# Wider channel-mixing spans and smaller fp32 tiles in a polynomial-attention mixer kernel

## The chip, the cores and the metric

One core of a Trainium2 chip runs the whole program. The metric is the device time of one execution in microseconds; the kernel before took 226.24 (median of 3 runs, 225.53 to 226.71). Five engines work side by side: TensorE (PE, with its weight loads listed apart as PEld), VectorE (DVE), ScalarE (ACT), GpSimd (POOL) and SyncE (SP), which issues the DMAs here.

## The reference

Attention with products of two learned projections in place of exponentials, followed by a mixer of tokens and channels. Batch is 4, heads 4, sequence 1088, head size 32, model width 128.

```
def phi(x):                                  # S1, S2: 8 x 32
    a = einsum('rd,bhsd->bhsr', S1, x)
    b = einsum('rd,bhsd->bhsr', S2, x)
    return outer(a, b).reshape(..., 64)
kv  = einsum('bhsf,bhsd->bhfd', phi(k), v)   # per head 64 x 32
z   = sum(phi(k), axis=2)
x   = einsum(phi(q), kv) / (einsum(phi(q), z) + 1e-6)
x   = x, heads side by side                  # B x 1088 x 128
h   = relu(x.T @ w_tok1) @ w_tok2            # tokens, 1088 -> 256 -> 1088
u   = x + h.T
out = u + relu(u @ w_ch1) @ w_ch2            # channels, 128 -> 1536 -> 128
```

## The kernel before

All work on features lies transposed, 128 model columns on the partitions. The four batches go one after the other through these steps; the planner names operations by step and batch (K1 is the keys of batch 1).

- **Weights.** The mixer's weights arrive as 64-bit floats in pieces of up to 512 columns. `convert` (lines 337 to 376) makes 32-bit words of each piece: two passes on ScalarE (L347, L351), three on VectorE (clamp L354, shift L358 by way of a PSUM bank of tag ps_h, merge L361) and an addition on GpSimd (L365, L367). `divide_weight` then splits the words into a high and a low fp32r half (L448 on ScalarE, L451 on GpSimd).
- **Keys, K.** L478 projects the keys: for each 64 rows one fp32 matmul, 64 weight columns, 64 columns of result. ScalarE copies one factor out (L488), VectorE multiplies the outer products (L497). L514 sums them against v with a column of ones: 64 features of one head as weights, the 66 columns of two heads as stream. L524 copies the wanted diagonal blocks into kvz, a block-diagonal matrix for two heads.
- **Queries, Q.** Batch 0 projects on PE with spread matrices (L593), and the product is made on VectorE (L614) or GpSimd (L611). Batches 1 to 3 project 16 rows per head (L559), write them to DRAM (L653), read them back repeated (L666, L669), and multiply in place (L679).
- **Attention and tokens, A.** L699 multiplies 64 tokens of phi(q) for two heads with kvz (66 columns). VectorE divides: L710 adds the small constant, L711 takes the reciprocal, L713 multiplies. Then come the token products (L749 in fp32 for batch 0, L755 in fp32r halves after it), relu, a transpose (L789), and the second product (L871, L875). u is split into halves uh and ul (L846, L849).
- **Channels, U.** The 4352 columns of all batches are cut in spans: 384, 384 and 320 for batch 0, then eight of 384 and one of 192 that run across batches. For each span and each of 12 pieces of 128 hidden channels, L925 makes the hidden values with three fp32r matmuls (high by high, high by low, low by high), ScalarE writes relu as the high half hh (L929), VectorE the rest hl (L932), and L938 adds three matmuls into the span's bank of tag ps_o. L957 or L963 adds u, and L974 stores.

An fp32 matmul appears in the trace as two passes, each with its weight load; one of fp32r as one. The buffers hid, hh and hl have four copies each, u, uh and ul four, the PSUM tags ps_a and ps_h three banks and ps_o two.

What runs when is settled ahead: `Plan.run` (lines 191 to 265) holds every operation with a cost per engine and picks, at each moment of its own clock, the ready operation with the highest level. The table LEAD raises or lowers some levels by hand, PBIAS keeps work off VectorE where GpSimd could take it, and gaps on PE longer than FILL are filled with matmuls of the identity (L326). Each engine then runs its own list in order.

The reason for splitting into spans is one line; another sets the attention's bank and columns:

```
for n in (384,) * 8 + (192,):
...
x_ps[c:c + 64, o:o + 2 * (D + 1)],
lhsT=qp[:, p, s0 + c:s0 + c + 64], rhs=kvz_all[b % 2][:, p, :], start=True, stop=True,
```

Of the kernel before, what the change touches and what calls it, by code (L numbers as in the profile page):

```python
# [18 lines left out]
P = 128  # L19
# [17 lines left out]
WIDE = 384  # L37


def _spans():  # L40
    spans = [((0, c0, cn),) for c0, cn in CHUNKS]
    at = S
    for n in (384,) * 8 + (192,):
        parts = []
        while n:
            b, c = divmod(at, S)
            m = min(n, S - c)
            parts.append((b, c, m))
            at, n = at + m, n - m
        spans.append(tuple(parts))  # L50
# [8 lines left out]
HID = 4  # L59
# [3 lines left out]
LEAD = {  # L63
    "A0.u2": -92200.0,
    "A0.ul00": 52700.0,
    "A0.x0": 25900.0,
    "A1.hT": -8500.0,
    "A2.t2": -139200.0,
    "A2.uh06": -39900.0,
    "A2.w1": 10800.0,  # L70
    "A3.t2": 42400.0,
    "A3.uh08": -24000.0,
    "A3.w1": -196200.0,
    "A3.x": -343500.0,
    "K0.c0": 176700.0,
    "K1.c0": 32500.0,
    "K2.c4": 181200.0,
    "Q0.p00": 649300.0,
    "Q0.p01": 151600.0,
    "Q0.p10": -11700.0,  # L80
    "Q0.p20": 167900.0,
    "Q0.p21": -40200.0,
    "Q1.m01": -15400.0,
    "Q3.p": -57100.0,
    "U0.f": 304500.0,
    "U1.f": 86500.0,
    "U11.f": 700.0,
    "U4.f": -200.0,
    "U6.f": -92300.0,
    "U7.f": -14400.0,  # L90
    "U8.f": -30200.0,
    "w00.hi": -545600.0,
    "w00.lo": -70200.0,
    "w01.hi": -76700.0,
    "w01.lo": -95600.0,
    "w02.add": -21200.0,
    "w02.clamp": -28000.0,
    "w02.hi": -51200.0,
# [12 lines left out]
    "w13.abs": 35300.0,
    "w13.clamp": -72500.0,
    "w13.hi": 21300.0,
    "w14.clamp": 29000.0,
    "w14.low": -26800.0,
    "w15.abs": -433000.0,
    "w15.clamp": 5100.0,
    "w15.low": -39400.0,
    "w20.abs": 69100.0,
    "w20.clamp": -38500.0,  # L120
    "w20.low": 61500.0,
    "w21.clamp": 7900.0,
    "w21.low": -32300.0,
    "w22.abs": -73200.0,
    "w22.low": -647900.0,
    "w30.abs": 8700.0,
    "w31.hi": -263000.0,
    "w32.abs": -118900.0,
    "w32.add": 25400.0,
    "w32.lo": -77700.0,  # L130
    "w32.low": -17200.0,
}
# [4 lines left out]
PBIAS = 1300.0  # L137
# [6 lines left out]
STICK = 3000.0  # L144
# [6 lines left out]
def f32(ap):  # L151
    return ap.bitcast(F32)
# [17 lines left out]
class Plan:  # L170
# [20 lines left out]
    def run(self, fill):  # L191
        for op in reversed(self.ops):
            cost = op.weight if op.weight is not None else min(op.ways.values()) + LATE.get(min(op.ways, key=op.ways.get), 0)
            op.level = cost + max((n.level for n in op.next), default=0.0)
        for op in self.ops:
            op.level += op.boost + LEAD.get(op.name, 0.0)
        free = dict.fromkeys(LATE, 0.0)
        free["sp"], free["act"], free["pe"] = 1060.0, 2000.0, 1400.0 + 427 * WARM
        dma, mode = 2800.0, 0

        port = 0.0
        waiting = {op: len(op.before) for op in self.ops}
        ready = [op for op in self.ops if not op.before]
# [6 lines left out]
        while ready:  # L210
            best = []
            for op in ready:
                t = max((a.end for a in op.after), default=0.0)
                ok = True
                for k, h in enumerate(op.takes):
                    q = self.taken.setdefault(h.pool, [])
# [7 lines left out]
                if not ok:  # L224
                    continue
# [819 lines left out]
```

## Time and profile before

| what | value |
|---|---|
| median of 3 runs | 226.24 us |
| span of the profiled execution | 224.5 us (its only time; the median lies 1.7 above) |
| busy: PE, DVE, ACT, POOL | 218.0, 142.7, 117.5, 80.0 us |
| granted TensorE clock | 1.00 (0.99 in the last 12.5 us) |
| moved by DMA | 28.41 MB, mean 127 GB/s |
| first channel-mixing pass | at 32.12 us |
| last matmul, last DVE instruction | start at 221.09 and 221.40 us |

In the chain of waits each row is a stretch: where it starts, how long it lasts, which engine's work it is, with the tile and line, and after an x how many instructions. A row of the timeline gives start, length, engine, line, operation, destination and sources, and in brackets how long the engine was idle before it and what ended that. A group row gives busy time and the mean of one instruction behind the bar. Busy time of PE is modelled where matmuls are pipelined, so the distance between starts says more than the length of one.

### The profile page before, as it was taken

The numbers are of one execution on the slowest core, as the hardware profiler recorded it, in microseconds if no ns is written. First come the engines' busy times: TensorE is split into PE (matmuls) and PEld (weight loads), VectorE is DVE, ScalarE is ACT, GpSimd is POOL, SyncE is SP. The second block draws the span as 40 slices with busy tenths as digits, with TensorE's granted clock in tenths as the row PEclk, the third lists the DMA queues.
The fourth block names the chain that finished last, engine by engine and source line by source line (L and its number), as shares of the span: only waits on it lengthen the run. The fifth ranks groups of instructions, "written<-read, shape, count | busy, mean of one in ns | idle before, by whom it ended". The sixth has DMA issues, their size and how long they took to land.

```text
span 224.5 us, 4803 instructions
## 1 busy us (share of the span) xinstructions
PE 218.0 (97%) x1860; PEld 204.5 (91%) x1860; DVE 142.7 (64%) x285; ACT 117.5 (52%) x271; POOL 80.0 (36%) x85
## 2 busy tenths in 40 slices
PE   7999999989999999999999999999999999999994
PEld 7667778869999999899999999999999999999994
DVE  1599989999578745366443755773375556556562
ACT  4597679986426153354443554343254554444451
POOL 2256589899997352243440230050020300000000
PEclk9999999999999999999999999999999999999999
DMA  5999995997419643038760000124000000101000
GB/s 175 418 404 403 405 355 173 208 197 233 156 33 220 196 158 105 32 67 202 222 206 3 3 35 0 38 105 105 3 35 1 35 3 2 33 0 39 0 35 18
DMA packets 10726, 28.41 MB, mean 127 GB/s; under 512 B 1360, under 2 KB 4688, under 8 KB 10704
## 3 DMA queue, kind: packets, MB, share of 16 engines
q1 hardware_dynamic: 10704, 28.11, 39.6%
q8 instruction: 14, 0.23, 0.4%
q14 instruction: 8, 0.07, 0.1%
HBM read 23.27 MB, written 4.83 MB: 125 GB/s over the span
## 4 chain that ended last, share of the span: by engine, by line
PE 78%; DMA 15%; DVE 3%; ACT 1%; SPq 1%; POOL 0%; issue 0%; POOLq 0%
PE ps_o L938 31%; PE ps_h L925 31%; DMA br<-rows 4%; PE ps_a L755 4%; DMA doubles<-wt 4%; PE ps_a L875 4%; DMA doubles<-wc 4%; PE ps_a L699 3%; DMA q_sb<-qT 3%; PE ps_a L514 2%; PE ps_a L871 1%; DVE hl L932 1%; PE ps_a L478 1%; DVE ps_h L358 1%; PE ps_o L326 0%; PE ps_a L789 0%
## 5 line engine op out<-in xcount | busy, mean ns | idle before, releaser
L932 DVE SCALAR_TENSOR_TENSOR hl<-ps_h,hh 128x384 fp32r<-128x384 f32 (+2 forms) x144 | 75.4, 533 | 53.6 <-ACT hh L929 53.3
L929 ACT ACTIVATE hh<-ps_h 128x384 fp32r<-128x384 f32 (+2 forms) x144 | 68.0, 474 | 69.4 <-PE ps_h L925 65.0
L925 PE MATMUL ps_h<-uh,halves 128*128 128x384 f32 (+2 forms) x288 | 89.8, 334 | 1.1 <-DVE hl L932 1.1
L938 PE MATMUL ps_o<-hh,halves 128*128 128x384 f32 (+2 forms) x288 | 71.7, 331 | 0.0
L925 PEld LDWEIGHTS ps_h<-uh,halves 128*128 128x128 f32 x288 | 53.6, 188 | 3.0 <-DVE hl L932 2.0
L938 PEld LDWEIGHTS ps_o<-hh,halves 128*128 128x128 f32 x288 | 50.5, 188 | 0.4
L925 PE MATMUL ps_h<-ul,halves 128*128 128x384 f32 (+2 forms) x144 | 47.5, 330 | 0.0
L938 PE MATMUL ps_o<-hl,halves 128*128 128x384 f32 (+2 forms) x144 | 47.3, 328 | 0.0
L925 PEld LDWEIGHTS ps_h<-ul,halves 128*128 128x128 f32 x144 | 27.1, 188 | 0.4 <-DVE ul L849 0.2
L938 PEld LDWEIGHTS ps_o<-hl,halves 128*128 128x128 f32 x144 | 27.1, 188 | 0.0
L849 POOL TENSOR_TENSOR ul<-us,uh 128x320 fp32r<-128x320 f32 (+5 forms) x15 | 9.4, 652 | 41.5 <-ACT uh L846 41.4
L679 POOL TENSOR_TENSOR qp<-qp,br 128x544 f32<-128x544 f32 x12 | 16.2, 1365 | 16.9 <-DMA br<-rows 16.9
L723 POOL TENSOR_TENSOR xl<-x,xh 128x384 fp32r<-128x384 f32 x9 | 9.1, 1016 | 20.4 <-ACT xh L719 20.4
L365 POOL TENSOR_TENSOR whole<-c,tail 128x512 int32<-128x512 int32 (+3 forms) x11 | 11.7, 1071 | 11.4 <-DVE c L361 11.4
L347 ACT ACTIVATE c<-doubles 128x512 f32<-128x512 f32 (+3 forms) x17 | 10.7, 627 | 4.0 <-POOL whole L365 2.6
L451 POOL TENSOR_TENSOR halves<-whole,halves 128x512 fp32r<-128x512 f32 (+3 forms) x11 | 11.8, 1093 | 0.2 <-ACT halves L448 0.2
L354 DVE TENSOR_SCALAR c<-c 128x512 f32<-128x512 f32 (+3 forms) x17 | 10.0, 612 | 2.9 <-ACT c L347 2.8
L497 DVE TENSOR_TENSOR k_p<-ps_a,a_sb 128x1024 f32<-128x1024 f32 (+1 forms) x12 | 10.9, 948 | 0.3 <-ACT a_sb L488 0.3
L699 PEld LDWEIGHTS ps_a<-kvz,qp 128*64 128x64 f32 x288 | 8.9, 137 | 1.9 <-issue 1.2
L361 DVE SCALAR_TENSOR_TENSOR c<-doubles,ps_h 128x512 int32<-128x512 int32 (+3 forms) x17 | 10.4, 610 | 0.2
L358 DVE TENSOR_SCALAR ps_h<-c 128x512 int32<-128x512 int32 (+3 forms) x17 | 10.2, 614 | 0.1
L351 ACT ACTIVATE tail<-doubles 128x512 int32<-128x512 uint32 (+3 forms) x17 | 10.0, 613 | 0.0
(76 smaller groups left out, 238.9 us busy)
## 6 DMA issues: line engine op xcount, KB each, us to landing
qp<-rows SPq DMA_DIRECT2D x6, 544.0 KB, 10.8
br<-rows SPq DMA_DIRECT2D x12, 272.0 KB
doubles<-wc SPq DMA_DIRECT2D x6, 512.0 KB, 9.5
v_sb<-v SPq DMA_DIRECT2D x4, 594.0 KB, 7.5
k_sb<-kT SPq DMA_DIRECT2D x4, 576.0 KB, 5.3
q_sb<-qT SPq DMA_DIRECT2D x4, 544.0 KB, 14.0
doubles<-wt SPq DMA_DIRECT2D x4, 512.0 KB, 9.8
xm<-xb SPq DMA_DIRECT2D x3, 576.0 KB, 2.8
```

Source lines behind the costliest of these rows:

```text
L347: nc.scalar.activation(f32(t["c"]), f32(high), AF.Abs)
L358: nc.vector.tensor_scalar(t["ps"], t["c"], 3, 0x3FFFFFFF, op0=ALU.logical_shift_left, op1=ALU.bitwise_and)
L361: nc.vector.scalar_tensor_tensor(t["c"], high, -(1 << 30), t["ps"], op0=ALU.bitwise_and, op1=ALU.bitwise_or)
L365: engines[e].tensor_tensor(dst(), t["c"], t["tail"], op=ALU.add)
L451: engines[e].tensor_tensor(halves[w, i][:, 1], f32(whole[w, i] if w < 2 else t["c"]), f32(halves[w, i][:, 0]), op=ALU.subtract)
L497: nc.vector.tensor_tensor(t["k_p"][:pn, t0 * H:t1 * H], a.unsqueeze(3).broadcast_to([pn, n, R, R]), t["sb", t0][:pn, :n].unsqueeze(2).broa ...
L679: engines[e].tensor_tensor(qp[:, p, cs], qp[:, p, cs], t["br"][:, p, cs], op=ALU.mult)
L699: nc.tensor.matmul(x_ps[c:c + 64, o:o + 2 * (D + 1)], lhsT=qp[:, p, s0 + c:s0 + c + 64], rhs=kvz_all[b % 2][:, p, :], start=True, stop=True,)
L925: nc.tensor.matmul(h_ps[:, :cn], lhsT=part(2, at[2][e][0], l, at[2][e][1] * P, P), rhs=r[:, :cn], start=(m == 0), stop=(m == 2))
L929: nc.scalar.activation(t["hh"][:, :cn], t["h"][:, :cn], AF.Relu)
L932: nc.vector.scalar_tensor_tensor(t["hl"][:, :cn], t["h"][:, :cn], 0.0, f32(t["hh"][:, :cn]), op0=ALU.max, op1=ALU.subtract)
L938: nc.tensor.matmul(outs[i][:, :cn], lhsT=part(3, at[3][e][0], l, at[3][e][1] * P, P), rhs=r[:, :cn], start=(e == 0 and m == 0), stop=(e == ...
```

## The change

It has four parts.

1. **Spans.** Behind batch 0 the spans are five of 512 and two of 352 columns in place of eight of 384 and one of 192. The buffers hid, hh, hl, u, uh and ul are 512 wide, with three copies instead of four.
2. **Smaller tiles for the fp32 products.** Every one of them now covers two or one heads with a part of PE's rows or columns. Key projection: 64 rows by 32 columns, 72 matmuls per batch instead of 18. Key sums: 32 features as weights and one head's 33 columns as stream, 72 instead of 36. Query projection of batches 1 to 3: 64 rows by 32 columns, 8 instead of 4; of batch 0: 64 rows by 128 columns, twice as many. kvz is no longer block-diagonal.
3. **Attention by single heads.** 64 rows by 64 columns, 33 columns of stream, 72 matmuls instead of 36; the two row halves write to two banks. Batches 1 to 3 take two sets of tiles (five and four) instead of three of three, on three banks of ps_a and one of ps_h; batch 0 keeps three sets, each with a bank of ps_a and one of ps_h. A division has two additions, one reciprocal and two multiplications instead of one each.
4. **Order.** The levels and LEAD are gone. A list, ORDER, names every operation in the order in which it is emitted, with the engine where there was a choice. Five of the twelve in-place query products and two low halves of weights, all on GpSimd before, are now on VectorE.

```
-WIDE = 384
+WIDE = 512
...
-    for n in (384,) * 8 + (192,):
+    for n in (512,) * 5 + (352, 352):
...
-HID = 4
+HID = 3
...
+ORDER = """
+s d00 q0 k0 d01 v0 d02 d03 d04 d10 d11 d20 d30 q1 d12 s.low s.abs s.clamp s.shift s.merge s.add Q0.s0:pool Q0.s1:dve s.rows w00.abs Q0.p00 Q0.p01
...
+        for entry in ORDER:
+            name, _, e = entry.partition(":")
+            op = named[name].pop(0)
+            e = e or next(iter(op.ways))
...
-                            t["ab", base][c:c + 64, (i - base) * 64:(i - base + 1) * 64],
-                            lhsT=box["k_sb", b][:, s0 + c:s0 + c + 64], rhs=f32(s_t["c"]), start=True, stop=True,
+                            t["ab", p][c:c + 32, i * 32:(i + 1) * 32],
+                            lhsT=box["k_sb", b][rows, s0 + c:s0 + c + 32], rhs=f32(s_t["c"])[rows, p * 32:(p + 1) * 32], start=True, stop=True,
...
-                            t["kv"][j * F:(j + 1) * F, p * 2 * (D + 1):(p + 1) * 2 * (D + 1)],
-                            lhsT=t["k_p"][:n, i * H + h].rearrange("p i j -> p (i j)"),
-                            rhs=t["v"][:n, i, 2 * p:2 * p + 2, :].rearrange("p h d -> p (h d)"),
+                                t["kv"][o:o + F // 2, p * (D + 1):(p + 1) * (D + 1)],
+                                lhsT=t["k_p"][:, p, i * 2 + j, c * R // 2:(c + 1) * R // 2].rearrange("p i j -> p (i j)"),
+                                rhs=t["v"][:, i, 2 * p + j, :],
...
-            nc.tensor.matmul(ps[j * 64:(j + 1) * 64, :QC], lhsT=box["s_rows"], rhs=q[:, c * QC:(c + 1) * QC], start=True, stop=True)
+                nc.tensor.matmul(ps[p][c * 32:(c + 1) * 32, :QC], lhsT=box["s_rows"][rows], rhs=q[rows, c * QC:(c + 1) * QC], start=True, stop=True)
...
-                nc.sync.dma_start(t["rows"][:, j * 2 * QC:(j + 1) * 2 * QC], t["abT"][j * 64:(j + 1) * 64].rearrange("p r c -> p (r c)"))
+                nc.sync.dma_start(t["rows"][j * 32:(j + 1) * 32].rearrange("f (c x) -> c f x", x=QC), t["abT"][:, j])
...
+        sets = ((0, 5), (5, 9)) if b else ((0, 3), (3, 6), (6, 9))
+        x_banks = [(Hold("ps_a"), Hold("ps_a" if b and a else "ps_h")) for a, z in sets]
...
-                                x_ps[c:c + 64, o:o + 2 * (D + 1)],
-                                lhsT=qp[:, p, s0 + c:s0 + c + 64], rhs=kvz_all[b % 2][:, p, :], start=True, stop=True,
+                                    ps[j][c:c + 64, o:o + D + 1],
+                                    lhsT=qp[rows, p, s0 + c:s0 + c + 64], rhs=kvz_all[b % 2][rows, p, :], start=True, stop=True,
...
+                for j in range(2):
+                    nc.vector.tensor_scalar_add(den[:, j], views[j][:, :, D], 1e-6)
                 nc.vector.reciprocal(rec, den)
+                xv = t["x"][:, t0:t1].rearrange("p t (a j) d -> p (t a) j d", j=2)
+                for j in range(2):
+                    nc.vector.tensor_tensor(xv[:, :, j], views[j][:, :, 0:D], rec[:, j].unsqueeze(2).broadcast_to([P, 2 * n_t, D]), op=ALU.mult)
```

Two places show what moves. The first is VectorE's list where the conversions end and channel mixing begins, in the kernel before; c is the piece in work, doubles with two digits names weight and piece, ul is the low half of the first span, hl the rest of the hidden values.

```order
L354 TENSOR_SCALAR c_434<-c_434 128x512
L354 TENSOR_SCALAR c_417<-c_417 128x384
L358 TENSOR_SCALAR ps_h_462<-c_434 128x512
L358 TENSOR_SCALAR ps_h_469<-c_417 128x384
L361 SCALAR_TENSOR_TENSOR c_434<-doubles30_90,ps_h_462 128x512
L849 TENSOR_TENSOR ul_473<-ps_a_437,uh_472 128x384
L361 SCALAR_TENSOR_TENSOR c_417<-doubles13_92,ps_h_469 128x384
L932 SCALAR_TENSOR_TENSOR hl_496<-ps_h_486,hh_495 128x384
```

The same place in the changed kernel; L293, L297 and L300 are clamp, shift and merge there, L799 makes ul and L882 hl.

```order
L300 SCALAR_TENSOR_TENSOR c_596<-doubles12_89,ps_h_608 128x384
L293 TENSOR_SCALAR c_612<-c_612 128x512
L297 TENSOR_SCALAR ps_h_648<-c_598 128x512
L297 TENSOR_SCALAR ps_h_650<-c_612 128x512
L300 SCALAR_TENSOR_TENSOR c_598<-doubles30_88,ps_h_648 128x512
L799 TENSOR_TENSOR ul_644<-ps_a_627,uh_643 128x384
L300 SCALAR_TENSOR_TENSOR c_612<-doubles31_92,ps_h_650 128x512
L799 TENSOR_TENSOR ul_660<-ps_a_635,uh_659 128x384
L293 TENSOR_SCALAR c_657<-c_657 128x512
L882 SCALAR_TENSOR_TENSOR hl_749<-ps_h_662,hh_748 128x384
```

Ahead of the first ul there are now eleven merged pieces of the mixer's weights instead of ten, and a twelfth is shifted; the second ul follows the first directly, ahead of any hl.

The second place is PE's list around the attention of batch 2, before: L925 and L938 are the two channel products of a span, L699 the attention.

```order
L925 MATMUL ps_h<-ul,halves_457 128x384
L925 MATMUL ps_h<-uh,halves_457 128x384
L699 MATMUL ps_a<-kvz_77,qp 64x66 x36
L938 MATMUL ps_o<-hh,halves_528 128x384 x2
L938 MATMUL ps_o<-hl,halves_528 128x384
```

The attention of batch 3 in the changed kernel, its first rows; L875 and L888 are the channel products there and L650 the attention.

```order
L888 MATMUL ps_o<-hh,halves_754 128x512 x2
L888 MATMUL ps_o<-hl,halves_754 128x512
L650 MATMUL ps_a<-kvz_78,qp 64x33
L650 MATMUL ps_h<-kvz_78,qp 64x33
L650 MATMUL ps_a<-kvz_78,qp 64x33
L650 MATMUL ps_h<-kvz_78,qp 64x33
```

One block of 36 matmuls into one tag became 72 that alternate between two banks, as the row half changes from one to the next; for the last four tiles both banks are of tag ps_a. Around the block the channel products are 512 columns wide.

More of the change, by code (lines that the diff above doesn't have):

```diff
@@ L191, in run @@
     def run(self, fill):
[L192 to L196, printed above, removed]
         free = dict.fromkeys(LATE, 0.0)
         free["sp"], free["act"], free["pe"] = 1060.0, 2000.0, 1400.0 + 427 * WARM
[L199 to L203, printed above, removed]
+        dma, mode, port = 2800.0, 0, 0.0
+        named = {}
+        for op in self.ops:
+            named.setdefault(op.name, []).append(op)
         def clock(s, cost):
@@ new lines, in run @@
+        for entry in ORDER:
+            name, _, e = entry.partition(":")
+            op = named[name].pop(0)
+            e = e or next(iter(op.ways))
+            cost = op.ways[e]
+            assert all(a.end is not None for a in op.before), entry
+            s = max([free[e]] + [a.end for a in op.after])
+            for h in op.takes:
+                q = self.taken.setdefault(h.pool, [])
+                n = self.bufs.get(h.pool, 1)
+                if len(q) >= n:
+                    s = max([s] + [u.end for u in q[len(q) - n].users])
+                q.append(h)
+            shared = e == "pool" or (e == "dve" and op.port)
+            if shared:
+                s = max(s, port)
+            f = s + cost
@@ L291, in attn_mixer_kernel @@
     engines = {"dve": nc.vector, "pool": nc.gpsimd, "act": nc.scalar}
-    bufs = {"c": 4, "tail": 4, "a_sb": 3, "ar": 3, "den": 2, "o_sb": 2, "q_sb": 2, "u": 4, "uh": 4, "ul": 4, "us": 2, "xb": 1, "xm": 2, "xT": 1, "rec": 2, "hid": HID, "hh": HID, "hl": HID, "rows": 2, "ps_a": 3, "ps_h": 3, "ps_o": 2}
+    bufs = {"c": 4, "tail": 4, "a_sb": 3, "ar": 3, "den": 2, "o_sb": 2, "q_sb": 2, "u": 3, "uh": 3, "ul": 3, "us": 2, "xb": 1, "xm": 2, "xT": 1, "rec": 2, "hid": HID, "hh": HID, "hl": HID, "rows": 2, "ps_a": 3, "ps_h": 3, "ps_o": 2}
     const = ctx.enter_context(tc.tile_pool(name="const", bufs=1))
@@ L565, in attn_mixer_kernel, with project_queries @@
-    s_rows_done = plan.add("s.rows", act_sb(64), rows_order, [s_done])
+            last = plan.add(
+                f"{n}.s{p}", {"pe": 18 * 38.0}, sums(p), [products[p], v_loaded[b]],
+                [] if p else [kv_hold], [kp_hold, v_hold[b]] + ([kv_hold] if p else []), boost, 5, order=[last],
+            )
+        return plan.add(n + ".kvz", {"act": 130.0}, blocks, [last], (), [kv_hold], boost)
+    def project_queries(q, ps):
+        for c in range(4):
+            for p in range(2):
+                rows = slice(p * 64, (p + 1) * 64)
+                nc.tensor.matmul(ps[p][c * 32:(c + 1) * 32, :QC], lhsT=box["s_rows"][rows], rhs=q[rows, c * QC:(c + 1) * QC], start=True, stop=True)
@@ L567, in queries_on_pe @@
+    def rows_order(_):
+        box["s_rows"] = const.tile([P, 32], F32, name="s_rows")
+        for p in range(2):
+            rows = slice(p * 64, (p + 1) * 64)
+            nc.scalar.copy(
+                box["s_rows"][rows].rearrange("p (k h r) -> p k h r", k=2, h=2),
+                f32(s_t["c"])[rows, p * 32:(p + 1) * 32].rearrange("p (h k r) -> p k h r", k=2, r=R),
+            )
+    s_rows_done = plan.add("s.rows", {"act": 300.0}, rows_order, [s_done])
     def queries_on_pe(qp_hold):
```

358 lines of the change are left out of this document (136 added, 222 removed).

## The prediction

> **What bounds the kernel now.** I read the page's busy shares and slices first.
>
> ```profile
> span 224.5 us, 4803 instructions
> PE 218.0 (97%) x1860; PEld 204.5 (91%) x1860; DVE 142.7 (64%) x285; ACT 117.5 (52%) x271; POOL 80.0 (36%) x85
> PE   7999999989999999999999999999999999999994
> DVE  1599989999578745366443755773375556556562
> POOL 2256589899997352243440230050020300000000
> PEclk9999999999999999999999999999999999999999
> ```
>
> PE is full in nearly every slice at a full granted clock, but a busy PE row also covers pipelined time, so I looked at stretches. Columns: PE, PEld, DVE, ACT, POOL busy, each with its instruction count, clock, DMA share, GB/s.
>
> ```profile
> 20.00:32.00 12.00, 11.22 (x103) 8.49 (x100) 11.42 (x29) 8.61 (x19) 7.88 (x8) 1.00 1.03 406
> 32.00:50.00 18.00, 16.93 (x178) 13.72 (x176) 17.04 (x30) 16.75 (x41) 16.78 (x15) 1.00 0.80 196
> 50.00:60.00 10.00, 10.00 (x146) 9.52 (x146) 7.70 (x12) 5.04 (x13) 9.77 (x9) 1.00 0.59 185
> 166.00:212.00 46.00, 46.00 (x268) 46.00 (x267) 25.72 (x49) 22.37 (x48) 1.77 (x4) 1.00 0.04 14
> ```
>
> There are three regimes. Up to 32 us PE waits for loaded and converted weights and VectorE is 95% busy. From 32 to 50 PE, VectorE, ScalarE and GpSimd are all 93 to 95% busy. From 50 us to the end PE has no gap: a microsecond taken from PE there is a microsecond off the end. In the third regime the chain of waits (start, length, work) prices every kind of block:
>
> ```profile
> 50.13 1.20 PE ps_a L478 x36
> 57.07 2.25 PE ps_a L514 x72
> 63.74 2.26 PE ps_a L699 x72
> 94.28 1.07 PE ps_a L559 x8
> 154.19 1.56 PE ps_h L925 x9
> 164.10 0.88 PE ps_a L875 x6
> 214.02 0.65 PE ps_h L925 x6
> 220.03 1.35 PE ps_o L938 x12
> ```
>
> These are key projection, key sums, attention, query projection, channel mixing at 384 columns, the second token product at 320 columns, and channel mixing at 192 columns (two rows). An fp32 matmul counts as two passes. The median of the runs, 226.24, lies 1.7 above this execution's span of 224.5; the sum below is made on that execution, and I carry the 1.7 over unchanged.
>
> **The change part by part.**
>
> *Spans.* A pass takes 1.56/9 = 173 ns at 384 columns and 0.88/6 = 147 ns at 320, so 0.415 ns per column: 226.5 ns at 512 and 160 ns at 352. At 192 columns it takes 0.65/6 = 108 to 1.35/12 = 112 ns, more than the 93 ns of that line, so I use 110. Each later span has 72 passes (12 pieces, 6 each). Before: 72 x (8 x 173.3 + 110) = 107.7 us; after: 72 x (5 x 226.5 + 2 x 160) = 104.6. Gain 3.2 us. If a pass grew in proportion to columns (231 ns at 512, 159 at 352) it would be 1.7.
>
> *Key sums.* 36 matmuls of 64 weight columns streaming 66 become 72 of 32 streaming 33, on four column tiles instead of two. The row gives 31 ns a pass with two tiles; halved in both widths and spread over four tiles it would be 7.8 ns, 1.13 us for 144 passes. The upper end is no gain, 2.25. I take 1.3, near the low end, since weights and stream both halve. Saving 0.95.
>
> *Key projection.* 36 passes become 144, of 32 by 32 on eight tiles. The same halving gives 0.6 us, no gain 1.2; I take 0.9, the middle, as no row shows eight tiles. Saving 0.3.
>
> *Query projection.* Eight passes of 272 columns on two tiles (134 ns each) become 16 on eight tiles: 16 x 134 x 2/8 = 0.54 us, at most 1.07. I take 0.6. Saving 0.45.
>
> *Attention.* 72 passes become 144 on four tiles. The stream halves (66 to 33 columns), but each weight load keeps 64 columns. If the stream sets the pace: 144 x 31/4 = 1.13 us. If the load does: 2.26, no gain. The 192-column rows show that a floor beside the stream exists, since 110 ns lies above the 93 ns of the line. They show it for loads of 128 rows by 128 columns; these loads fill half the rows. So neither end has a row of its own. I take 1.4, nearer the lower, since stream and rows halve and the tiles double, and the floor is shown for the whole array only. Saving 0.86 a block.
>
> [...]
>
> *Which savings count.* Only those of the third regime: attention of batches 1 to 3 (2.6), sums of batches 2 and 3 (1.9), key projections of 2 and 3 (0.6), the last query projection (0.45). Those of batch 0, and K1 and Q2 before 50 us, lie beside a busy VectorE; if it stopped covering them they would add up to 1.7 more. The faster query projection of batch 0 is covered by the conversions as well.
>
> *The first 50 us.* Work moves onto VectorE.
>
> ```profile
> 24.28 0.17 DVE L710 TENSOR_SCALAR den<-ps_a 128x12 f32<-128x12 f32 x1
> 24.48 0.23 DVE L711 RECIPROCAL rec<-den 128x12 f32<-128x12 f32 x1
> 24.75 0.56 DVE L713 TENSOR_TENSOR x<-ps_a,rec 128x384 f32<-128x384 f32 x1
> 25.68 0.41 DVE L354 TENSOR_SCALAR c<-c 128x512 f32<-128x512 f32 x1
> 26.48 0.68 DVE L358 TENSOR_SCALAR ps_h<-c 128x512 int32<-128x512 int32 x1
> 27.20 0.69 DVE L361 SCALAR_TENSOR_TENSOR c<-doubles,ps_h 128x512 int32<-128x512 int32 x1
> 31.80 0.56 DVE L849 TENSOR_TENSOR ul<-ps_a,uh 128x384 fp32r<-128x384 f32 x1 [0.21 <-ACT uh L846]
> 32.12 0.42 PE L925 MATMUL ps_h<-uh,halves 128*128 128x384 f32 x1
> L614 DVE TENSOR_TENSOR qp<-xT,ps_h 128x384 f32<-128x384 f32 (+1 forms) x3 | 1.6, 532 | 1.1 <-PE ps_h L593 1.1
> L451 POOL TENSOR_TENSOR halves<-whole,halves 128x512 fp32r<-128x512 f32 (+3 forms) x11 | 11.8, 1093 | 0.2 <-ACT halves L448 0.2
> L679 POOL TENSOR_TENSOR qp<-qp,br 128x544 f32<-128x544 f32 x12 | 16.2, 1365 | 16.9 <-DMA br<-rows 16.9
> 216.71 0.33 ACT L929 ACTIVATE hh<-ps_h 128x192 fp32r<-128x192 f32 x1 [0.34 <-PE ps_h L925]
> 217.07 0.36 DVE L932 SCALAR_TENSOR_TENSOR hl<-ps_h,hh 128x192 fp32r<-128x192 f32 x1 [0.31 <-ACT hh L929]
> ```
>
> VectorE costs (0.56 - 0.36)/192 = 1.04 ns a column. Batch 0's three divisions go from 0.17 + 0.23 + 0.56 = 0.96 us to 2 x 0.17 + 0.23 + 2 x 0.36 = 1.29: +1.0 in all. Two 544-column products leave GpSimd (1.37 each) for VectorE: 0.53 at 384 (the mean 532 ns), so 0.70 each, +1.4. Two low halves of weights (512 and 384 columns) move likewise, +1.2; one copy of 256 columns, +0.4. Together +4.0 on VectorE, and 2 x 1.37 + 2 x 1.09 = 4.9 off GpSimd. The new order also puts one whole piece more (0.41 + 0.68 + 0.69 = 1.8 us) ahead of the first ul, so channel mixing starts some 2 to 3 us after 32.12, but with two spans ready. Conversions only change places, so what counts is the added work: VectorE has 1.0 us free between 32 and 50. The bounds are -1.1 (PE's own idle of that stretch goes) and +3.0. GpSimd, as full as VectorE there, is relieved by more than VectorE gains, and PE has less to do: I take +0.8, the lower middle.
>
> *The tail.* The last addition and store grow from 192 to 352 columns:
>
> ```profile
> 221.09 0.27 PE L938 MATMUL ps_o<-hl,halves 128*128 128x192 f32 x1
> 221.40 0.35 DVE L963 TENSOR_TENSOR o_sb<-us,ps_o 128x192 f32<-128x192 f32 x1 [0.62 <-PE ps_o L938]
> SPq L974 <- DVE o_sb L963: 101.1, 9, 15.0
> ```
>
> VectorE +0.17, the transfer of 176 KB instead of 96 a little: +0.3 (0.2 to 0.6). Query rows written in pieces half as long, and stores of other widths, go through SyncE, which waits 101 us in all for results to store: I cost them at nothing, and at one late product of 1.37 us if the rows come late.
>
> *Sum.* 226.24 - 3.2 - 2.6 - 1.9 - 0.6 - 0.45 + 0.8 + 0.3 = **218.6 us**.
>
> **The rivals.**
>
> *Slower: a floor per pass.* Passes leave PE in order; where each takes about 31 ns whatever its size, twice or four times as many small ones cost more. For it: L478, L514 and L699 all come to 31 to 33 ns a pass, with 64 columns as with 66. Against it are passes that share time. One fp32 pass of 384 columns alone takes (8.88 - 8.23)/2 = 0.325 us:
>
> ```profile
> 8.23 0.81 PE L593 MATMUL ps_h<-q_sb,s_spread 128*128 128x384 f32 x2
> 8.88 0.70 PE L593 MATMUL ps_a<-q_sb,s_spread 128*128 128x320 f32 x2
> ```
>
> At 272 columns that is 230 ns, and L559, on two tiles, needs 134. Price, after 50 us: attention 144 x 31 = 4.5 instead of 2.26, three times, +6.7; sums +4.5; keys +6.6; the query projection +1.1; spans -3.2, the rest +1.1: 243.0 us. It decides from the point where the mean pass of these seven blocks (1008 passes, 13.7 us before, 2.5 us of other gains to lose) exceeds 16 ns; the forecast has 8.5. Chance 0.07.
>
> [...] No run here has a stream below 64 columns.
>
> *Attention gains nothing,* its loads being the pace: 218.6 + 2.6 = 221.2. For it, the floor at 192 columns. Chance 0.18.
>
> *The first 50 us cost all that VectorE gets,* +3.0 instead of +0.8: 220.8; with attention's loss too, 223.4. Chance 0.08.
>
> *The loop becomes latency-bound,* with three buffers instead of four.
>
> ```profile
> 204.16 0.34 PE L925 MATMUL ps_h<-uh,halves 128*128 128x384 f32 x1
> 204.54 0.49 ACT L929 ACTIVATE hh<-ps_h 128x384 fp32r<-128x384 f32 x1 [0.55 <-PE ps_h L925]
> 205.06 0.56 DVE L932 SCALAR_TENSOR_TENSOR hl<-ps_h,hh 128x384 fp32r<-128x384 f32 x1 [0.48 <-ACT hh L929]
> 205.73 0.33 PE L938 MATMUL ps_o<-hl,halves 128*128 128x384 f32 x1
> ```
>
> From the last first-product pass at 204.16 to the pass that needs hl at 205.73 PE does nine passes, and hl is ready at 205.62: 0.11 us to spare. At 512 columns nine passes are 2.04 us and the chain 0.43 + 0.60 + 0.03 + 0.69 = 1.75: 0.29 to spare. So this eases; it needs a lost 0.13 us in each of 60 wide steps to eat 7.6 us. Chance 0.02, with 226 to 228. That the gains are as large as forecast and nothing shows (another wait takes their place): 225 to 227, chance 0.03.
>
> **How the numbers follow.** Forecast 0.62. Low end: all gains at their best (attention 0.8 more, sums 0.35, keys 0.6, early blocks 1.7, the first 50 us 1.9): 213.2. High end: attention without gain and the whole VectorE cost, 223.4, rounded up. Range **213 to 224**. A difference of 0.5% (1.1 us) is about what can be told from no change. Faster: 0.62 + 0.18 + 0.08 less 0.02 for combinations, 0.86; same 0.05; slower 0.09.
>
> **What would show it.** Passes of 512 columns at 226 ns; sums near 1.3 us, attention at 1.1 to 1.5 (2.2 names the load, 4 the floor per pass), keys under 1. First channel pass between 33 and 36 us, PE without a gap from about 53. Wrong would be: gaps on PE released by hl or ul after 55 us, or small blocks longer than before.

## The result, and the profile after

The changed kernel takes 238.95 us (median; 238.59 to 243.82) against 226.32 us for the kernel before beside it: a ratio of 1.056 (95% interval 1.054 to 1.059). The forecast was 218.6 us. It is 12.6 us slower where 7.6 us less were expected. The profiled execution has a span of 237.2 us.

The page of the changed kernel, its busy shares, the slices and the instruction queue of TensorE (packets, MB, share):

```profile
span 237.2 us, 6580 instructions
PE 220.0 (93%) x2790; PEld 191.4 (81%) x2790; DVE 149.2 (63%) x281; ACT 109.4 (46%) x234; POOL 65.3 (28%) x64
PE   7984999789888999998999999989999999999994
DVE  1593649979996866685562694548644446466553
PEclk9996569999999999999999999999999999999999
q8 instruction: 22, 0.36, 0.6%
```

Two things were not there before: a hole in TensorE's row in the fourth slice, and a granted clock of about half its value in slices 4 to 6. VectorE has holes in the same place, though it was forecast to be what the first 50 us wait for. The same stretches as before, with one more at the hole:

```profile
16.00:22.00 6.00, 1.39 (x95) 1.21 (x82) 3.89 (x7) 1.97 (x6) 1.16 (x1) 0.81 1.02 404
20.00:32.00 12.00, 10.68 (x179) 10.13 (x179) 5.76 (x23) 2.93 (x7) 4.37 (x5) 0.50 0.72 284
32.00:50.00 18.00, 15.26 (x226) 11.86 (x225) 13.64 (x24) 12.43 (x27) 9.23 (x9) 0.96 0.67 203
```

From 16 to 22 us TensorE works 1.39 of 6 us while the DMA engines are full (1.02). From 20 to 32 it is busy again, at a clock of 0.50, and VectorE works 5.76 us instead of 11.42: it waits for TensorE now (5.6 us of it in one wait, for the attention of batch 0). TensorE's timeline shows where this begins (start, length, work, idle time ahead and its releaser):

```profile
15.36 1.35 PE L453 MATMUL ps_o<-v_sb,k_p 128*32 128x33 f32 x135
21.32 0.37 PE L453 MATMUL ps_o<-v_sb,k_p 128*32 128x33 f32 x9 [4.62 <-issue]
21.62 2.50 PE L265 MATMUL ps_o<-ident 128*128 128x128 f32 x10
28.45 3.78 PE L265 MATMUL ps_o<-ident 128*128 128x128 f32 x16
44.26 0.63 PE L875 MATMUL ps_h<-uh,halves 128*128 128x384 f32 x1
48.53 0.29 PE L418 MATMUL ps_a<-s_c,k_sb 64*32 64x32 f32 x15 [1.01 <-issue]
```

Batch 0's key sums stop after 135 of 144 passes for 4.62 us, and the reason given is "issue": nothing that the profile shows is waited for. The first channel-mixing pass comes at 44.26 us instead of 32.12. From there to the end of the span it is 192.9 us, and it was 192.4 before. So the whole 12 us are lost ahead of channel mixing, and behind it the change gains nothing on balance. The blocks behind it, in busy time of the block alone, before (attention, key sums, key projection) and after (attention of batches 1 and 2, key sums, key projection):

```profile
60.00:85.00 25.00, 2.33 (x72) 2.19 (x72) 1.00 0.57 160
55.00:62.00 7.00, 2.32 (x72) 2.18 (x72) 1.00 0.46 170
48.00:53.00 5.00, 1.27 (x36) 1.13 (x36) 1.00 0.86 208
```

```profile
60.00:85.00 25.00, 2.30 (x144) 2.19 (x144) 1.00 0.47 145
95.00:120.00 25.00, 2.60 (x144) 2.37 (x144) 1.00 0.40 111
146.00:152.00 6.00, 1.43 (x144) 1.32 (x144) 1.00 0.01 3
95.00:105.00 10.00, 1.42 (x144) 1.31 (x144) 1.00 0.41 134
```

Attention gains 0.03 us in batch 1 instead of 0.86 (in batches 2 and 3 it takes 2.60 and 2.59, with a short idle inside the block), key sums gain 0.89 (forecast 0.95), key projection loses 0.15 instead of gaining 0.3. The chain of waits adds the other prices and the waits that are new:

```profile
81.34 0.62 PE ps_a L492 x16
106.16 1.53 issue
146.93 1.40 PE ps_h L875 x6
157.59 0.68 issue
```

The query projection takes 0.62 us, as forecast (0.6). A 512-column pass takes 1.40/6 = 233 ns, not 226.5. Two more waits for "issue" lie in dense blocks of small passes.

**What "issue" is.** The packets on q8 carry instructions, 0.36 MB in 22 packets, 16 KB each, and their number follows TensorE's. It runs 2 x 2790 instructions (a weight load and a matmul a pass), about 254 a packet; before it was 2 x 1860 in 14 packets, 266 a packet. So a packet is a page of some 128 passes. At the 31 ns a pass of the kernel before, a page of key sums lasts 4 us; at 8.6 ns (1.24 us for 144) it lasts 1.1 us.

### The profile page after: what moved, and what is told of

Its sections match the earlier page's. It is cut to its first block, busy times and chain, and to the rows that moved or that the text cites. A ratio compares the mean times of both kernels' runs of the same rounds, so it can differ in the third digit from the quotient of the medians.

```text
span 237.2 us, 6580 instructions
## 1 busy us (share of the span) xinstructions
PE 220.0 (93%) x2790; PEld 191.4 (81%) x2790; DVE 149.2 (63%) x281; ACT 109.4 (46%) x234; POOL 65.3 (28%) x64
## 4 chain that ended last, share of the span: by engine, by line
PE 84%; issue 6%; DVE 5%; ACT 2%; POOL 1%; POOLq 0%; ACTq 0%
PE ps_h L875 29%; PE ps_o L888 28%; PE ps_o L265 6%; PE ps_a L650 4%; PE ps_a L705 4%; PE ps_a L825 4%; PE ps_a L418 2%; PE ps_a L453 1%; DVE c L293 1%; DVE c L300 1%; PE ps_a L532 1%; DVE ps_h L297 1%; DVE qp L627 1%; PE ps_h L532 1%; PE ps_a L492 1%
## 5 line engine op out<-in xcount | busy, mean ns | idle before, releaser
L882 DVE SCALAR_TENSOR_TENSOR hl<-ps_h,hh 128x512 fp32r<-128x512 f32 (+3 forms) x120 | 72.0, 608 | 60.7 <-ACT hh L879 59.9
L879 ACT ACTIVATE hh<-ps_h 128x512 fp32r<-128x512 f32 (+3 forms) x120 | 63.9, 535 | 80.4 <-PE ps_h L875 53.0
L875 PE MATMUL ps_h<-uh,halves 128*128 128x512 f32 (+3 forms) x240 | 81.0, 365 | 1.1 <-DVE c L300 1.1
L888 PE MATMUL ps_o<-hh,halves 128*128 128x512 f32 (+3 forms) x240 | 68.2, 365 | 0.0
L875 PEld LDWEIGHTS ps_h<-uh,halves 128*128 128x128 f32 x240 | 44.6, 188 | 7.0 <-DVE c L300 1.4
L888 PEld LDWEIGHTS ps_o<-hh,halves 128*128 128x128 f32 x240 | 43.0, 188 | 6.1 <-issue 0.7
L888 PE MATMUL ps_o<-hl,halves 128*128 128x512 f32 (+3 forms) x120 | 43.3, 360 | 1.6 <-DVE hl L882 1.6
L875 PE MATMUL ps_h<-ul,halves 128*128 128x512 f32 (+3 forms) x120 | 43.2, 360 | 0.0
L799 POOL TENSOR_TENSOR ul<-us,uh 128x256 fp32r<-128x256 f32 (+6 forms) x9 | 6.7, 748 | 72.8 <-ACT uh L796 64.2
L888 PEld LDWEIGHTS ps_o<-hl,halves 128*128 128x128 f32 x120 | 22.6, 188 | 4.6 <-DVE hl L882 1.9
L875 PEld LDWEIGHTS ps_h<-ul,halves 128*128 128x128 f32 x120 | 22.6, 188 | 2.4
L265 PE MATMUL ps_o<-ident 128*128 128x128 f32 x88 | 16.3, 360 | 1.4 <-POOL ident masks.py:199 1.4
L265 PEld LDWEIGHTS ps_o<-ident 128*128 128x128 f32 x88 | 15.2, 268 | 1.6 <-POOL ident masks.py:199 1.4
L293 DVE TENSOR_SCALAR c<-c 128x512 f32<-128x512 f32 (+3 forms) x17 | 10.1, 605 | 5.8 <-ACT c L286 5.7
L650 PEld LDWEIGHTS ps_a<-kvz,qp 64*64 64x64 f32 x384 | 11.0, 151 | 2.3 <-issue 1.8
L650 PE MATMUL ps_a<-kvz,qp 64*64 64x33 f32 x384 | 11.8, 234 | 0.8 <-issue 0.7
L300 DVE SCALAR_TENSOR_TENSOR c<-doubles,ps_h 128x512 int32<-128x512 int32 (+3 forms) x17 | 10.3, 608 | 0.1
L297 DVE TENSOR_SCALAR ps_h<-c 128x512 int32<-128x512 int32 (+3 forms) x17 | 10.2, 615 | 0.1
```

What stands on the lines that cost most here:

```text
L265: nc.tensor.matmul(spare_ps[:, :P], lhsT=ident, rhs=ident, start=True, stop=True)
L293: nc.vector.tensor_scalar(f32(t["c"]), f32(t["c"]), LEAST, MOST, op0=ALU.max, op1=ALU.min)
L297: nc.vector.tensor_scalar(t["ps"], t["c"], 3, 0x3FFFFFFF, op0=ALU.logical_shift_left, op1=ALU.bitwise_and)
L300: nc.vector.scalar_tensor_tensor(t["c"], high, -(1 << 30), t["ps"], op0=ALU.bitwise_and, op1=ALU.bitwise_or)
L650: nc.tensor.matmul(ps[j][c:c + 64, o:o + D + 1], lhsT=qp[rows, p, s0 + c:s0 + c + 64], rhs=kvz_all[b % 2][rows, p, :], start=True, stop=True,)
L875: nc.tensor.matmul(h_ps[:, :cn], lhsT=part(2, at[2][e][0], l, at[2][e][1] * P, P), rhs=r[:, :cn], start=(m == 0), stop=(m == 2))
```

## The experiments

*Theory A:* TensorE runs out of instructions. Its pages come through the DMA engines, behind the loads of weights up to 32 us; small passes use a page up before the next arrives, and the idle halves the clock (0.50 from 20 to 32 us). *Theory B:* the new order is late by itself. *Theory C:* the small tiles are slow in themselves. Spans, attention and keys have questions of their own.

### Batch 0 in half as many passes

The three pieces are key projection, key sums and attention; kvd_all is the block-diagonal form of kvz_all.

```
-                for c in range(0, n, 32):
+                w = 64 if b in (0,) else 32
+                for c in range(0, n, w):
...
-                        for c in range(2):
+                        parts = 1 if b in (0,) else 2
+                        for c in range(parts):
...
+                            if b in (0,):
+                                at_ = i - t0
+                                o = (2 * (at_ % 3) + p) * 2 * (D + 1)
+                                nc.tensor.matmul(
+                                    ps[at_ // 3][c:c + 64, o:o + 2 * (D + 1)],
+                                    lhsT=qp[:, p, s0 + c:s0 + c + 64], rhs=kvd_all[b % 2][:, p, :], start=True, stop=True,
+                                )
+                                continue
```

> The changed kernel, order and spans untouched; in batch 0 alone key projection, key sums and attention go back to half as many passes (64-column tiles, and for attention the block-diagonal right side of 66 columns), 72 passes each instead of 144. Theory A (TensorE waits for its instructions: twice the passes use up a 16 KB page of instructions before the next one, queued behind the loads of weights, arrives; the idle then halves the granted clock): no idle of 4 to 5 us between 16 and 22 us, granted clock above 0.9 in 20 to 32 us, first channel-mixing pass at 33 to 37 us instead of 44.3, time 229 to 232 us. Theory B (the new order is late by itself, whatever the tiles): first channel-mixing pass at 41 us or later, 236 to 239 us. Theory C (the small tiles are slow in themselves): the three blocks get shorter by 1 us each at most and the start moves by 1 to 3 us, the idle stays.

Measured: 227.15 us, a ratio of 1.006 (1.003 to 1.010) to the kernel before. Two rows of its timeline, then the stretch of the hole:

```profile
14.80 2.29 PE L459 MATMUL ps_o<-v_sb,k_p 128*64 128x33 f32 x72
34.35 0.64 PE L910 MATMUL ps_h<-uh,halves 128*128 128x384 f32 x1
```

```profile
16.00:22.00 6.00, 6.00 (x132) 5.77 (x129) 5.86 (x13) 3.75 (x10) 3.73 (x4) 1.00 1.02 415
```

No hole, full clock, channel mixing at 34.35 us, in the very order that Theory B blames: B falls. C falls too, since the blocks themselves differ by a microsecond and the start by ten. The time is 2 us below A's number, since the stalls behind the start are nearly gone as well: no wait of TensorE is put down to issue any more, though one of 1.08 us put down to hh, ending at 89.07 us, also stands at a page's border (after 1241 passes, 1457 of the changed kernel up to there less 216; pages are counted further below). The key sums here stream 33 columns but load 64 weight columns, and take 2.29 us, as before (2.32): halving the stream alone brings nothing.

### The kernel before with nothing but batch 0's key sums cut

```
+                        if b in (0,):
+                            for c in range(2):
+                                o, x = j * F + c * F // 2, (2 * p + j) * (D + 1)
+                                nc.tensor.matmul(
+                                    t["kv"][o:o + F // 2, x:x + D + 1],
+                                    lhsT=t["k_p"][:n, i * H + h, c * R // 2:(c + 1) * R // 2].rearrange("p i j -> p (i j)"),
+                                    rhs=t["v"][:n, i, h, :], start=(i == 0), stop=(i == NT - 1),
+                                )
+                            continue
```

> The kernel before, its planner, order, spans and all other tiles kept; only the key sums of batch 0 are cut as in the change (32-column weights, 33-column streams, 144 passes instead of 72). Theory A: the page of instructions is used up while the next one waits behind the weights' loads, so the kernel before shows the stall too: an idle of 1 to 4 us put down to issue between 15 and 22 us, granted clock below 1.0 up to 32 us, first channel-mixing pass 1 to 8 us after 32.1, time 227 to 234 us. Theory B (the new order is to blame): no idle, the block 1 us shorter, 225 to 226 us.

Measured: 228.75 us, a ratio of 1.010 (1.006 to 1.014). Two rows of its timeline, then the stretch from 20 to 32 us:

```profile
19.79 0.31 PE L517 MATMUL ps_o<-v_sb,k_p 128*32 128x33 f32 x10 [2.90 <-issue]
34.83 0.42 PE L934 MATMUL ps_h<-uh,halves 128*128 128x384 f32 x1
```

```profile
20.00:32.00 12.00, 11.85 (x124) 9.20 (x114) 8.90 (x23) 7.11 (x17) 6.10 (x6) 0.86 1.03 407
```

One block made faster by a microsecond puts the same hole into the kernel before, with its own order, and costs 2.7 us.

### The loads moved away from the hole

Of the order's lines only the part that changes is shown; the six loads stood in its first line.

```
-Q0.a11 K0.kvz w02.low
+Q0.a11 K0.kvz d10 d11 d20 d30 q1 d12 w02.low
...
+            if name == "d10":
+                nc.scalar.copy(to[:, 0:1].bitcast(F32), kvz_all[0][:, 0, 0:2])
```

> The changed kernel, every tile and pass kept; the loads d10 d11 d20 d30 q1 d12 are issued only once kvz of batch 0 is there (a copy of one element into the first one's target makes it wait), so the data queues are nearly empty while the key sums of batch 0 run. Theory A (an instruction page is late because it queues behind the data): the idle inside the key sums of batch 0 shrinks from 4.6 us to 1 to 1.5 us, the fetch of one page on empty queues; the granted clock stays above 0.9 up to 25 us; the weights then come later by 6 to 8 us, so the first channel-mixing pass lies anywhere from 37 to 44 us. Theory B (order): the idle stays at 4 to 5 us, and the start is later than 44.3 us by what the loads are late, 46 to 50. Theory C: the idle stays.

Measured: 245.21 us, but with a scatter from 237.91 to 247.38, so no ratio. What counts is its trace: timeline, and all DMA from 15 to 20 us in 40 slices.

```profile
15.90 1.35 PE L456 MATMUL ps_o<-v_sb,k_p 128*32 128x33 f32 x135
19.48 0.28 PE L456 MATMUL ps_o<-v_sb,k_p 128*32 128x33 f32 x9 [2.23 <-issue]
50.40 0.36 PE L421 MATMUL ps_a<-s_c,k_sb 64*32 64x32 f32 x15 [4.78 <-issue]
```

```profile
DMA  0000000000000000040000000000000000000000
DMA packets 1, 0.02 MB, mean 3 GB/s; under 512 B 0, under 2 KB 0, under 8 KB 0
q8 instruction: 1, 0.02, 1.2%
```

The hole shrinks from 4.6 to 2.2 us, at the same pass of the same block. With the DMA engines otherwise empty, the one packet of these 5 us is the page, in the slice at 17.1 us, when TensorE stops; TensorE goes on 2.3 us after the packet's start. In the changed kernel TensorE stops at 16.71 us and the packet starts between 18.8 and 18.9 us:

```profile
q8 instruction: 1, 0.02, 67.4%
```

There TensorE goes on 2.5 us after the packet's start, nearly as on empty queues: behind the loads it is the packet's start that comes 2 us late. Counted from the moment when TensorE enters the page before (after its first 222 passes, 15.4 us there, 16.0 us here), the next page is ready after 5.9 us behind the loads and after 3.5 us on empty queues. The hole is longer than the 1 to 1.5 us expected. The first channel-mixing pass, at 42.16 us, lies where it was expected; the granted clock, 0.66 from 20 to 25 us, does not. The key projection of batch 1, where the loads now run, stops for 4.8 us instead of 1.0. The stall follows the traffic, as only Theory A has it.

### Batch 0's keys in few passes, its attention in many

The first two edits of the first experiment, without the third.

> The changed kernel with key projection and key sums of batch 0 in half as many passes, as in the run before, but attention of batch 0 in its 144 passes of 64 by 64. Theory A (TensorE waits for an instruction page): the instruction at which it stood now comes some 288 instructions later in the program, near the end of batch 0's attention, where 256 instructions again go by in about 2 us while the data queues are still full. The idle of 2 to 5 us moves from the key sums into the attention of batch 0 (18 to 25 us), the granted clock falls again, first channel-mixing pass at 37 to 43 us, time 231 to 238 us. Theory A' (only the key sums matter, as their tiles collide in some way): no such idle, first channel-mixing pass at 34 to 35 us, 227 us.

Measured: 234.69 us, a ratio of 1.035 (1.031 to 1.040); the profiled execution, 237.6, is the slowest of four. Two rows of its timeline:

```profile
23.11 0.24 PE L652 MATMUL ps_a<-kvz,qp 64*64 64x33 f32 x1 [1.62 <-issue]
46.87 0.69 PE L877 MATMUL ps_h<-ul,halves 128*128 128x384 f32 x1 [4.27 <-issue]
```

The stall moved into attention, smaller than expected (1.6 us), and channel mixing begins at 38.9. A second one of 4.3 us sits behind the dense key projection of batch 1, where none was expected.

Where these waits lie is settled by counting TensorE's passes from the start of the program to each of them. The rows are the changed kernel up to its hole, the kernel before with batch 0's key sums cut, this run up to its second wait, and the run without fillers (next) up to a wait of 2.56 us; the first count of a row is that of the passes:

```profile
0.00:17.50 17.50, 15.29 (x351) 12.57 (x351) 10.00 (x19) 10.15 (x23) 5.89 (x12) 1.00 0.89 337
0.00:18.00 18.00, 15.52 (x222) 12.02 (x222) 10.97 (x21) 12.26 (x28) 5.67 (x13) 1.00 0.90 340
0.00:44.00 44.00, 37.56 (x604) 31.50 (x604) 32.04 (x69) 25.65 (x57) 20.16 (x25) 0.96 0.88 314
0.00:26.50 26.50, 17.93 (x479) 14.30 (x479) 16.13 (x36) 13.15 (x30) 9.25 (x15) 0.85 0.94 365
```

The holes come after 222, 351, 479 and 604 passes. The later ones of the changed kernel (1.01, 1.53 and 0.68 us) come after 732, 1624 and 2390, that of 4.78 us with late loads after 732, and this run's first one after 351. From one count to the next it is 125 to 129 passes or a multiple of that, a page each time (the counts leave out TensorE's few other instructions). So every hole stands at the border of a page, whatever block is at work there, and the second hole of this run does too.

### Without the fillers

```
-        if len(plan.taken["ps_o"]) < 3:
+        if len(plan.taken["ps_o"]) < 3 and not box.get("keys"):
```

> The changed kernel with its late instruction page kept, but without the filler transposes behind the first key projection (they compute nothing that is used). Theory A says that 4.6 us of idle become 12 us of delay since the granted clock is halved and everything behind, fillers (8 us at that clock) included, runs in order at half pace: without the fillers the first channel-mixing pass comes at 39 to 42 us instead of 44.3, though idle time may keep the clock low longer; time 234 to 239. If the conversions on VectorE and ScalarE set the start whatever TensorE does: 44 us as before, the fillers' time turned into idle.

Measured: 234.19 us, a ratio of 1.038 (1.034 to 1.042), channel mixing from 39.58 us. The stall is still there, split over three page borders: 0.56, 1.85 and 2.56 us, after 223, 351 and 479 passes. So the 56 fillers left out (16 ahead of the stall, 40 behind it: 10, 16, 10 and 4) cost 4.7 of the 12 us on balance: the order puts them where its planned times see idle, and after the stall they run ahead of the work behind them, 26 of the 40 at half the clock. The rest of the delay is the stall and the half clock (0.50 from 20 to 32 us here too).

### Attention with twice the stream

The changed part of the line:

```
-rhs=kvz_all[b % 2][rows, p, :]
+rhs=kvz_all[b % 2][rows, p, :].unsqueeze(1).broadcast_to([F, 2, D + 1]) if b else kvz_all[b % 2][rows, p, :]
```

> The changed kernel; in batches 1 to 3 each attention pass streams 66 columns instead of 33 (the same 33 twice), weights, tiles and number of passes kept. If the weight loads set attention's pace: a block stays at 2.1 us (up to 2.3), time within 1 us of the changed kernel's 239. If the stream sets it: a block takes 3 to 4.2 us, time 242 to 245. If a floor per pass does: unchanged as well, but then 72 passes with the same tiles would take half, which the block of before (2.1 us with 72 passes) already speaks against.

Measured: 239.64 us (237.86 to 241.48), as the changed kernel. The attention of batches 2 and 3, which lie at full or nearly full clock, in busy time of the block:

```profile
95.00:120.00 25.00, 2.58 (x144) 2.44 (x144) 0.93 0.37 102
150.00:165.00 15.00, 2.66 (x144) 2.38 (x144) 1.00 0.01 3
```

The changed kernel has 2.60 and 2.59 there. Twice the stream costs at most 0.07 us a block: the weight loads set the pace. Batch 1's block took 3.94 us in this execution, but at a clock of 0.66 (from 69 to 74 us), so it is not compared.

### Attention and key projection in half as many passes, all batches

The first and the third edit of the first experiment for all four batches.

> The changed kernel with attention (block-diagonal right side, 66 columns) in 72 passes and key projection in 72 passes (64-column tiles) in all four batches; key sums and query projection stay new in all four, batch 0's sums too. If the weight loads set the pace: attention 2.1 to 2.3 us a block and key projection 1.0 to 1.3 us, no gain and no loss by itself against 144 passes; if a floor per pass does: 1.1 and 0.6 us, some 4 us less in all. Theory A: batch 0's key sums alone still use 288 instructions within 1.3 us, but 144 fewer lie ahead of them; an idle of 1 to 5 us may stay in them or go; later idle times put down to issue (1.0, 1.5 and 0.7 us in the changed kernel) are gone but for those in key sums. Time 226 to 228 us without the idle in batch 0, 230 to 236 with it.

Measured: 227.58 us, a ratio of 1.008 (1.005 to 1.010). Attention and key projection in busy time of the block:

```profile
60.00:70.00 10.00, 2.33 (x72) 2.19 (x72) 1.00 0.46 155
84.00:96.00 12.00, 1.25 (x72) 1.14 (x72) 1.00 0.47 146
```

Attention takes 2.33 us in 72 passes and 2.30 in 144: no fixed cost per pass, since half the passes would then take half. Key projection takes 1.25 in 72 passes on four tiles and 1.42 in 144 on eight, so the smaller tiles, with twice the passes, lost time. A hole of 2.5 us put down to issue stays, just behind batch 0's key sums and again after 351 passes; channel mixing begins at 37.76 us. The time is nevertheless inside the 226 to 228 us that were expected without a hole, so a hole of this length costs less than expected (see the last pair of runs). This run is 11 us faster than the changed kernel although its blocks take about the same time: what went is idle time and half clock (0.86 from 20 to 32 us instead of 0.50).

### Spans alone

```
-    for n in (384,) * 8 + (192,):
+    for n in (512,) * 5 + (352, 352):
...
-HID = 4
+HID = 3
```

> The kernel before with the spans alone: 512 five times and 352 twice instead of 384 eight times and 192, three buffers instead of four for the tiles that grow; its order is made by the same planner with the new costs. By the prediction's straight line (226 ns a 512-column pass): -3.2 us, 223.1. By the pass that the changed kernel's trace shows (236 ns): -0.5 to -1.0, 225.3 to 225.8. If three buffers or the later first span cost the loop: slower than 227.

Measured: 238.26 us, a ratio of 1.055 (1.052 to 1.057), far from every number expected. The planner of the kernel before makes another order with these spans, and two of TensorE's largest waits are for batch 3's mixer (uh) and for hl:

```profile
PE ps_h L925 <- ACT uh L846: 3.2, 1, 3.2
PE ps_h L925 <- DVE hl L932: 1.8, 2, 1.5
```

They are 5.0 of the 12 us; the rest was not taken apart. So this run says nothing of a span's price. That it comes near the changed kernel's time is chance: runs with the same spans in the new order take 222 to 227 us. The price is read from rows, that of 352 columns from the chain of the last run below:

```profile
195.70 0.96 PE ps_h L910 x6
```

A pass of 352 columns takes 160 ns, as forecast, so the spans bring 107.7 - 72 x (5 x 0.233 + 2 x 0.160) = 0.8 us. A run of the old spans in the new order was not tried.

### Two parts that pay, on the kernel before

Key sums of batches 1 to 3 as in the second experiment, and the query projections of batches 1 to 3 as in the change.

> The kernel before, its planner and spans kept; the key sums of batches 1 to 3 and the query projections of batches 1 to 3 are cut as in the change, nothing else. By the blocks of the changed kernel's trace (sums 1.24 us instead of 2.25, queries 0.62 instead of 1.07) where TensorE has no gap: -1.9 to -2.9 and -0.45 to -1.35 us, 222 to 224 us. If each dense block of 144 passes runs out of instructions once (1.0 to 1.5 us), the sums' gain is eaten: 225 to 226 us.

Measured: 224.30 us, a ratio of 0.992 (0.990 to 0.994), 0.3 us above the expected range, with 2.3 us of waits for hl where the kernel before has 1.1. No wait for issue shows. A block of 144 passes is little longer than a page of some 128, and longer passes (173 ns at 384 columns) share its pages; how long each page lasted is not shown, since no stall marks the borders here. That none came late is in part luck of where the borders fall: in the changed kernel the key sums of batch 2 stopped for 1.53 us, those of batches 1 and 3 not at all.

### The changed kernel with only what pays

The edits of the first experiment: attention and key projection for all batches, key sums for batch 0. The second of the pair moves two products back (the changed part of one line is shown).

```
-Q1.m01:dve w32.lo:dve Q1.m11:dve
+Q1.m01:pool w32.lo:dve Q1.m11:pool
```

> The changed kernel's order and spans; attention and key projection in 72 passes in all batches and the key sums of batch 0 in 72 passes too, so that only the spans, the query projections and the key sums of batches 1 to 3 are new. Theory A: no instruction page is late any more: no idle put down to issue above 0.5 us, granted clock 1.00 from 10 us on, first channel-mixing pass at 34 to 35 us, and with sums of 1.24 us and the two waits for VectorE (1.6 and 0.3 to 0.9 us) that the order brings 223.5 to 225.5 us. Theory B (the order itself costs more than those waits): 226 us or more.

> The kernel of the run beside it, with two products of the queries of batch 1 (544 columns each) moved from VectorE back to GpSimd, where the kernel before has them. If VectorE, that takes 1.4 to 1.8 us for each while GpSimd works instead of the 0.7 forecast, makes TensorE wait 1.6 us for hl: this wait goes, 1 to 1.6 us less. If GpSimd then brings the last product late: a wait of 1 to 2.5 us of the attention of batch 1 takes its place, same or slower by 1 us.

Measured: 224.43 us, a ratio of 0.995 (0.992 to 0.997), and 222.04 us, a ratio of 0.983 (0.981 to 0.985). The first has its channel mixing from 34.48 us and no wait for issue. It differs from the run in half as many passes, all batches, in batch 0's key sums alone, and is 3.2 us faster: that is what the hole of 2.5 us cost there. Its one large wait is the first row below, and VectorE just before it is the rest (two products of 1.36 and 1.80 us, and a low half between), here as the changed kernel's timeline shows the same group:

```profile
PE ps_o L923 <- DVE hl L917: 1.6, 1, 1.6
```

```profile
66.45 1.36 DVE L627 TENSOR_TENSOR qp<-qp,br 128x544 f32<-128x544 f32 x1
67.73 1.50 DVE L390 TENSOR_TENSOR halves<-c,halves 128x512 fp32r<-128x512 f32 x1
69.15 1.80 DVE L627 TENSOR_TENSOR qp<-qp,br 128x544 f32<-128x544 f32 x1
71.87 0.44 PE L888 MATMUL ps_o<-hl,halves 128*128 128x384 f32 x1 [1.62 <-DVE hl L882]
```

In the second the wait is gone and no wait of attention takes its place. It is 2.4 us faster than the first, where 1 to 1.6 were expected; the wait explains 1.6 of them. It is 1.7% faster than the kernel before. Its later VectorE products take 717 ns each (next row); in the changed kernel the same three, at 104.09, 136.63 and 140.64 us, take 715 to 720 ns, and GpSimd does nothing beside them; in the rows above GpSimd worked without a gap from 65.0 to 73.0 us.

```profile
L639 DVE TENSOR_TENSOR qp<-qp,br 128x544 f32<-128x544 f32 x3 | 2.1, 717 | 0.0
```

## Why the prediction was wrong

- **The step that failed** is "*The first 50 us*. Work moves onto VectorE ... I take +0.8", and with it the line that batch 0's savings "lie beside a busy VectorE". It counted only what the engines do and took 33 to 36 us for the first channel pass; it came at 44.3. The cost was not on VectorE: 2 x 930 more instructions on TensorE, densest where the DMA queues are full (a share of 1.02 from 16 to 22 us), stopped it for 4.6 us, halved its clock (0.50 from 20 to 32 us), and 40 fillers then ran ahead of the work behind them. Without the stall the same order starts at 34.35 us, inside the forecast. The rivals looked at how long a pass lasts, at VectorE and at the buffers, none at how a pass gets to the engine; a row that could have raised the question stood on the page (14 packets on q8 for 1860 passes). "PE without a gap from about 53" failed for the same reason: two more page borders, 1.53 and 0.68 us.
- **Attention** "1.4, nearer the lower" was wrong: 2.30. The other end, 2.26, named as the load's pace, holds: 144 loads on four tiles start within 2.1 us, which gives 58 ns for 64 columns on each tile, and twice the stream adds at most 0.07 us. The rival "attention gains nothing" was right about its block.
- **Key projection** 0.9 was wrong: 1.42 busy, 0.15 above before. "The same halving", 0.6 us, would need 4 ns a pass; on eight tiles the passes come about 8.6 ns apart, the same as key sums on four tiles.
- **Key sums** 1.3 was right (1.24 from the first start to the last, 1.43 with the last pass's tail), and so was the **query projection** (0.62).
- **Spans**: the straight line fell short by 7 ns at 512 columns, 72 x 5 x 6.5 = 2.3 us of the 3.2.
- **VectorE's products**: "0.70 each" held beside an idle GpSimd (717 ns); beside a busy one they took 1.36 and 1.80, and TensorE waited 1.6 us.
- **The floor-per-pass rival** came to 243.0, near the time, by luck: 144 passes of key sums start 8.6 ns apart, far under its 16 ns, and those of attention 14.6 ns. The passes, on different tiles, overlap: a single weight load is recorded with 109 ns in key sums and 135 ns in attention (medians).

The terms, by the traces: 218.6, + 11.3 for the start (12.1 instead of 0.8), + 2.5 attention, + 0.9 key projection, + 2.3 spans, + 2.7 waits for VectorE (1.6 for hl and 1.1 for a conversion), + 3.2 later stalls (1.0, 1.5 and 0.7), - 1.2 for batch 1's sums and queries, which the forecast left out, - 1.1 for before's own waits for hl: 239.2 us, measured 238.95. The sum is bookkeeping; shown by experiment are the stall, its place at a page's border, its dependence on passes and on traffic, the fillers' share, the load as attention's pace and the wait behind the two products. Not settled are the scatter of the run with late loads, of which one execution was traced, and why the clock stayed at half so long.

## What to carry over

Count the instructions of a change as well as their durations: where TensorE's passes get short, divide its instructions by the 254 that a page held here and compare the time that a page lasts with the 3.5 us measured on empty queues, or with the 5.9 us measured where loads fill the DMA engines (a share of 1.02). A smaller tile paid where it halved the weight columns with twice the passes (key sums, 2.32 to 1.43 us; query projection, 1.07 to 0.62), and not with four times the passes (key projection, 1.27 to 1.42) or where only the stream or the rows are halved (attention, 2.33 to 2.30). An early idle can cost more than itself, since the clock fell after it and an order fixed ahead keeps its fillers: 4.6 us cost 12 in the changed kernel (clock 0.50 from 20 to 32 us), though 2.9 us cost 2.7 in the kernel before (0.86).

## What the hardware showed that was not expected

- TensorE's next page was ready 3.5 us after TensorE had entered the page before on empty queues, and 5.9 us after it behind full ones (DMA share 1.02); a page of key sums lasts 1.1 us, and TensorE stood still for 2.2 and 4.6 us. A page held 254 instructions in the changed kernel, and the holes lie 125 to 129 passes apart, or a multiple of that.
- After 4.6 us without work the granted clock stood at 0.50 for 10 us and more, though TensorE was busy in them (10.00 of 10.00 us from 22 to 32):

```profile
22.00:32.00 10.00, 10.00 (x170) 9.52 (x169) 5.73 (x22) 2.67 (x6) 4.37 (x5) 0.50 0.66 261
```

- Passes on different tiles start 8.6 ns apart with 32 weight columns on four tiles (key sums; 4 x 8.6 = 34 ns a load on each) and 14.6 ns apart with 64 (attention; 4 x 14.6 = 58 ns a load, for 64 rows as for the 128 rows of before, where two tiles give 29 ns a pass); on eight tiles (key projection, 32 columns) they start 8.6 ns apart too.
